# Attention with a distance bias and a gated MLP on one core: the first two steps share one side of PSUM, shared steps move in odd groups, weight rows load earlier

## Chip, cores and metric

The kernel runs on 1 core of one Trainium2 chip. The metric is the device time of one execution in microseconds. Engines are named as in the profile: PE is TensorE (PEld its weight loads), DVE VectorE, ACT ScalarE, POOL GpSimd, SP SyncE, which here only issues DMAs.

## The reference

Two parts follow each other: attention over 4 batches x 8 heads x 576 positions x 64, with an additive bias that a small network makes from the distance of two positions, and an MLP over the 2304 tokens whose activation is a rational function.

```python
# attention, q, k, v: (4, 8, 576, 64)
scores = scale * np.matmul(q, k.transpose(0, 1, 3, 2))
x = (log1p(|i - j|) / log1p(max(i, 1)))[..., None]
h = np.maximum(x @ w1 + b1, 0.0)              # 32 hidden
bias = h @ w2                                 # 8 heads
attn = softmax(scores + bias.transpose(2, 0, 1)[None])
x = (attn @ v)  ->  (2304, 512)
# MLP: w_in (512, 2048), w_out (2048, 512), a[4], b[2]
h = x @ w_in
g = (a[0] + a[1]*h + a[2]*h**2 + a[3]*h**3) / (1 + |b[0]|*|h| + |b[1]|*h**2 + 1e-6)
out = g @ w_out
```

## The kernel before

**The table.** The bias depends on i and j only. 36 groups of 16 rows i are made one after the other (list `order`): VectorE and ScalarE make up to four rows of relu(w1 * l + b1) for each (`relu`, from the table `lts` of logarithms, scaled by w1 at L709), TensorE multiplies them with w2 (L761) into two of the eight PSUM banks (`pa`), ScalarE evicts them (`e`, L767), and SyncE stores `e` into `tab` in device memory (L772). `load_bias(p, c)` (L260) reads the bias of head pair p and row block c back from `tab[c]`, in three DMAs, six for c = 4.

**Attention.** A unit u is a pair of heads p of one batch b; there are 16. A unit has row blocks c = 0 to 3 of 128 rows, and the last 64 rows of units u and u + 1 together are one shared step (u, 4). `steps` lists them; nine steps, those of units u and u + 1, are a group: steps 9g to 9g + 8 are group g. Two steps i = 2r and i + 1 are one round r (`rnd`), r from 1 to 35. In a round TensorE makes, in this order, the scores of both steps (`e_qk`, L341), the transposes of the probabilities of the two steps before (`e_tp`, L425), and the products with v (`e_pv`, L484) of steps i - 3 and i - 2. VectorE takes scores and bias to a reduced tile with `e_ttr` (L357), copies the tails of the transposes (L452) and the outputs (L493); ScalarE makes exponentials (`e_exp`, L373) and copies the transposes (L440). `side(i)` says which four banks the scores of a step use. Steps 0 and 1 are started inside the table (`start`).

**What lies beside it.** While attention runs, `job_plan` splits the weights into a high and a low part, one job for each part of 128 rows or columns, a job every one and a half rounds: `load` (wx, L140, 512 KB) by SyncE, then steps on VectorE (wk, L156), ScalarE and GpSimd (L177, L188), then stores. wx has four buffers. `load_qk`, `load_v` and `load_bias` are called from `loads(i)`. When a unit's last step is through, its sums are inverted, copied out (rs, L462) and read back as `rb` (L392), and `e_norm` (L408) multiplies the unit's output by it, on GpSimd, for units 12 and 15 on VectorE, and stores it (L410). `done_to` says when.

**What sets the order.** The order on each engine is written out by hand: every engine and SyncE's queue do their instructions in program order. After round 35 and `finish` the MLP runs with matmuls alone on TensorE.

Of the kernel before, what the change touches and what calls it, by code (L numbers as in the profile page):

```python
# [9 lines left out]
F32 = mybir.dt.float32  # L10
F32R = mybir.dt.float32r
U32 = mybir.dt.uint32
AF = mybir.ActivationFunctionType
ALU = mybir.AluOpType
# [23 lines left out]
def tile_attn_moe(  # L38
# [194 lines left out]
    with tc.manual_schedule():  # L233
# [3 lines left out]
        with ExitStack() as actx:  # L237
# [84 lines left out]
            for u in range(2, len(units), 2):  # L322
                steps += [(u, c) for c in range(5)] + [(u + 1, c) for c in range(4)]
            s2, prob, pt, tl, xs = {}, {}, {}, {}, {}
            rsum, rb = {}, {}

            def side(i):
                return 4 * ((max(i // 2, 1) - 1 + i) % 2)

# [180 lines left out]
            def loads(i):  # L510
                g, c = divmod(i, UPG)
                for u, x, y in ((2 * g + 2, 0 if g else 4, 3 if g else 6), (2 * g + 3, 5 if g else 7, 8)):
                    if u < NU and c == x:
                        load_qk(u)
                    if u < NU and c == y and u != 3:
                        load_v(u)
                if i == UPG + 1:
                    load_v(3)
                p, r = divmod(i, 2 * UPG)
                r = {2: 0, 7: 1, 11: 2, 13: 3, 16: 4}.get(r)  # L520
                if r is not None and p + 1 < NP:
                    load_bias(p + 1, r)
                if i == NS - 18:
                    load_x(0, 0, 0, KD - 1)
                if i == NS - 5:
                    load_x(1, 1, 0, KD - 1)
# [3 lines left out]
            def done_to(k):  # L530
                g, c = divmod(k, UPG)
                u = 2 * g - 2
                if g > 0:
                    if c == (0 if g > 1 else 1) and u != NX or k == NS:
                        norms.extend(e_norm(u))
                    if c == 6 and g * 2 < NU:
                        norms.extend(e_norm(u + 1))
                    if c == 2 and u + 1 < NU - 1:
                        load_rb(u + 1)
                if k == NS - 8:  # L540
                    x12.append(xs[NX])
                    late.extend(e_norm(NX))
                if g < NU // 2 and c == (7 - g % 2 if g else 8):
                    load_rb(2 * g)
# [15 lines left out]
            def job_plan(r):  # L560
# [10 lines left out]
                def out(c):  # L571
                    def go():
                        jobs[c][3][3](False, True)
                        run(list(after.get(c, [])))
                        if c + 3 < len(jobs):
                            jobs[c + 3][0]()
                    return go
# [12 lines left out]
            def rnd(r):  # L590
# [27 lines left out]
                for x in plan["between"]:  # L618
                    op = x()
                for x in plan["pool2"]:  # L620
                    behind(x(), op)
                small = [ends[r] + ends_[r] + adds[r] for r in range(2)]
                weave(main[0][:4] + small[0] + main[0][4:] + main_[0], main[1] + small[1] + main_[1])
                copy(1, 2)
                copy(0, 1)
# [9 lines left out]
                for x in hi[:1]:  # L635
                    x()
                for k in (i, i + 1):
                    for j in range(2):
                        e_exp(k, j)
                recip(i - 2)  # L640
# [6 lines left out]
                done_to(i - 1)  # L647
                run(late)
                loads(i + 1)
                if r == 2:  # L650
                    for x in jobs[:3]:
                        x[0]()
# [35 lines left out]
            with ExitStack() as bctx:  # L688
# [7 lines left out]
                bts = tpool.tile([P, NG * 4], F32, tag="bts", name="bts")  # L696
                LCUT = 320
                nc.scalar.dma_start(out=cs, in_=cst)
                nc.sync.dma_start(out=lts[:, :LCUT], in_=ltab[:, :LCUT])
                nc.sync.dma_start(out=lts[:, LCUT:], in_=ltab[:, LCUT:])  # L700
# [6 lines left out]
                A.activation(out=w28, in_=cs[:, 8 + 5 * NG:], func=AF.Identity, scale=8.0)  # L707
                for a, z in ((0, LCUT), (LCUT, S)):
                    V.tensor_scalar(  # L709
                        out=lts[:, a:z], in0=lts[:, a:z], scalar1=w1s, scalar2=None, op0=ALU.mult  # L710
                    )
                for x in range(9):
                    on(T.matmul(W[:, 6, 0:P], ident, ident, start=True, stop=True), 6)  # L713
# [12 lines left out]
                def relu(n):  # L726
                    for c, e in enumerate(ENG[n]):
                        r = ring[nring[0] % len(ring)][:, :dist(n)]
                        nring[0] += 1
                        m = 4 * n + c  # L730
                        if e == "A":
                            A.activation(out=r, in_=lts[:, :dist(n)], func=AF.Relu, bias=bts[:, m:m + 1])
# [10 lines left out]
                for n in order[:LEAD]:  # L743
                    relu(n)
                for y, n in enumerate(order):
                    if y == 13:
# [4 lines left out]
                    mid = i0 + NROW - 1  # L751
                    pa = 2 * ((y if y >= NG - 2 else y + 2) % 4)
                    pa = (pa, pa + 1)
                    cuts = sorted({0, mid, 512, EW})
                    for a, z in zip(cuts, cuts[1:]):
# [10 lines left out]
                    o = 512 * pa[0]  # L766
                    on(A.activation(  # L767
                        out=e, in_=WF[:, o:o + EW], func=AF.Identity, scale=rts[:, n:n + 1]
                    ), *pa)
                    g, k = divmod(n, 8)  # L770
# [309 lines left out]
```

## Time and profile before

| | |
|---|---|
| median of 3 plain runs | 660.62 us (660.62 to 661.08) |
| profiled execution, own time | 662.25 us |
| profiled execution, span | 660.5 us |
| mean granted TensorE clock | 0.999 |
| PE busy | 653.5 us, 99% |
| DVE busy | 561.3 us, 85% |
| ACT busy | 472.2 us, 71% |
| POOL busy | 154.1 us, 23% |
| all DMAs | 118.98 MB, 117.79 of them on one queue |

The span runs from the first to the last instruction; 1.75 us lie around it in the profiled execution. The end of a matmul is modelled in these profiles, so a busy PE may still be stretched. The chain of waits that ended last lies on PE for 96% of the span.

### The profile page before, as it was taken

The numbers are of one execution on the slowest core, as the hardware profiler recorded it, in microseconds if no ns is written. First come the engines' busy times: TensorE is split into PE (matmuls) and PEld (weight loads), VectorE is DVE, ScalarE is ACT, GpSimd is POOL, SyncE is SP. The second block draws the span as 40 slices with busy tenths as digits, with TensorE's granted clock in tenths as the row PEclk, the third lists the DMA queues.
The fourth block names the chain that finished last, engine by engine and source line by source line (L and its number), as shares of the span: only waits on it lengthen the run. The fifth ranks groups of instructions, "written<-read, shape, count | busy, mean of one in ns | idle before, by whom it ended". The sixth has DMA issues, their size and how long they took to land.

```text
span 660.5 us, 16193 instructions
## 1 busy us (share of the span) xinstructions
PE 653.5 (99%) x6274; PEld 546.8 (83%) x6274; DVE 561.3 (85%) x1100; ACT 472.2 (71%) x758; POOL 154.1 (23%) x108
## 2 busy tenths in 40 slices
PE   9999999999999999999999999999999999999997
PEld 6657888888888878988888888989988888888996
DVE  7997889988988895899999989979769779687776
ACT  7988999999999987767667566576656555555551
POOL 0000233333433330122212121222221221212211
PEclk9999999999999999999999999999999999999999
DMA  7887878868987975452825607669431301312031
GB/s 242 294 310 226 273 240 266 259 228 231 321 277 226 330 238 167 156 187 72 264 97 164 229 21 249 214 207 318 146 111 49 129 0 65 110 42 86 1 113 48
DMA packets 74845, 118.98 MB, mean 180 GB/s; under 512 B 11904, under 2 KB 33808, under 8 KB 74768
## 3 DMA queue, kind: packets, MB, share of 16 engines
q1 hardware_dynamic: 74624, 117.79, 54.2%
q8 instruction: 49, 0.80, 0.5%
q14 instruction: 28, 0.23, 0.1%
q10 hardware_dynamic: 144, 0.16, 0.1%
HBM read 79.17 MB, written 35.61 MB: 174 GB/s over the span
## 4 chain that ended last, share of the span: by engine, by line
PE 96%; DMA 1%; ACT 1%; issue 1%; DVE 0%; SPq 0%; POOL 0%; DVEq 0%; ACTq 0%; POOLq 0%
PE ps L316 30%; PE ps L909 30%; PE ps L484 12%; PE ps L341 11%; PE ps L761 6%; PE ps L425 6%; DMA tab<-e 1%; DMA bias<-tab 1%; PE ps L713 1%; ACT pt L440 1%; ACT p L373 1%; DVE s L357 0%; SPq L260 0%; DVE pre L930 0%; ACT wh L165 0%
## 5 line engine op out<-in xcount | busy, mean ns | idle before, releaser
L879 POOL TENSOR_TENSOR gl<-m,r 128x1024 fp32r<-128x1024 f32 (+1 forms) x39 | 85.6, 2195 | 295.5 <-DVE m L872 255.7
L830 ACT ACTIVATE w<-ps,babs 128x1024 f32<-128x1024 f32 (+1 forms) x40 | 41.3, 1033 | 107.1 <-PE ps L316 103.4
L373 ACT ACTIVATE p<-s,m 128x576 f32<-128x576 f32 x144 | 110.5, 783 | 0.2 <-DVE m L357 0.2
L357 DVE CUSTOM_DVE_ANT_0 s<-ps,bias 128x576 f32<-128x576 f32 (+1 forms) x144 | 95.2, 682 | 10.1 <-PE ps L341 3.9
L440 ACT COPY pt<-ps 128x512 f32<-128x512 f32 (+1 forms) x109 | 71.9, 732 | 17.6 <-PE ps L425 17.0
L909 PE MATMUL ps<-wol,gh 128*128 128x512 f32 x216 | 84.2, 390 | 0.0
L909 PE MATMUL ps<-woh,gh 128*128 128x512 f32 x216 | 84.2, 390 | 0.0
L341 PE MATMUL ps<-k,q 64*128 64x288 f32 (+1 forms) x640 | 82.3, 418 | 0.4 <-ACT e L767 0.2
L842 DVE SCALAR_TENSOR_TENSOR u<-w,babs,ps 128x1024 f32<-128x1024 f32 (+1 forms) x40 | 46.9, 1172 | 38.1 <-ACT t L831 38.0
L484 PE MATMUL ps<-pt,v 128*64 128x128 f32 (+1 forms) x1280 | 78.2, 265 | 0.8 <-ACT pt L440 0.5
L484 PEld LDWEIGHTS ps<-pt,v 128*64 128x64 f32 x1280 | 65.1, 137 | 5.8 <-ACT pt L440 1.6
L316 PE MATMUL ps<-xb,wih 128*128 128x512 f32 (+1 forms) x240 | 68.8, 367 | 0.0
L341 PEld LDWEIGHTS ps<-k,q 64*128 64x128 f32 (+1 forms) x640 | 50.9, 175 | 20.8 <-issue 6.4
L837 ACT ACTIVATE u<-u 128x1024 f32<-128x1024 f32 (+1 forms) x40 | 39.1, 978 | 40.2 <-DVE u L842 40.0
L425 PEld LDWEIGHTS ps<-ident,p 64*128 64x128 f32 x1296 | 49.6, 138 | 8.7 <-DVE m L357 2.9
L858 DVE SCALAR_TENSOR_TENSOR gh<-t,cst,r 128x1024 fp32r<-128x1024 f32 (+1 forms) x40 | 47.0, 1174 | 9.3 <-ACT r L839 6.9
L909 PE MATMUL ps<-woh,gl 128*128 128x512 f32 x216 | 53.8, 389 | 0.0
L425 PE MATMUL ps<-ident,p 64*128 64x64 f32 x1296 | 51.8, 226 | 0.5 <-ACT p L373 0.2
L865 DVE SCALAR_TENSOR_TENSOR m<-u,qc,gh 128x1024 f32<-128x1024 f32 (+1 forms) x40 | 47.1, 1178 | 4.0
L316 PEld LDWEIGHTS ps<-xb,wih 128*128 128x128 f32 x240 | 44.5, 188 | 6.1
L872 DVE SCALAR_TENSOR_TENSOR m<-t,cst,m 128x1024 f32<-128x1024 f32 (+1 forms) x40 | 47.1, 1179 | 1.4
L851 DVE SCALAR_TENSOR_TENSOR t<-t,cst,ps 128x1024 f32<-128x1024 f32 (+1 forms) x40 | 47.0, 1175 | 1.4
(82 smaller groups left out, 1343.9 us busy)
## 6 DMA issues: line engine op xcount, KB each, us to landing
tab<-e SPq DMA_DIRECT2D x36, 295.5 KB, 3.5
wx<-in_w_in_dram SPq DMA_DIRECT2D x16, 512.0 KB, 5.4
wx<-in_w_out_dram SPq DMA_DIRECT2D x16, 512.0 KB, 4.2
v<-in_vp_dram SPq DMA_DIRECT2D x16, 320.0 KB, 6.3
ws<-wh SPq DMA_DIRECT2D x20, 256.0 KB, 4.7
ws<-wl SPq DMA_DIRECT2D x20, 256.0 KB, 4.3
q<-in_qt_dram SPq DMA_DIRECT2D x16, 288.0 KB, 4.1
k<-in_kt_dram SPq DMA_DIRECT2D x16, 288.0 KB, 3.3
```

What stands on the lines that cost most here:

```text
L316: on(T.matmul(hps[s][:, j, :w_], w[:, k, sl], x[:, k, :w_], start=(k == 0 and z == 0), stop=(k == KD - 1 and z == 2),), b + j)
L341: on(T.matmul(W[o, b, :SH], q[r, x], k[r, a * SH:(a + 1) * SH], start=True, stop=True), b)
L357: op = on(V.tensor_tensor_reduce(out=t3[:, a], in0=W[:, b:b + 2][:, a, :SH], in1=b3[:, a], scale=-0.125, scalar=least, op0=ALU.add, op1=AL ...
L373: A.activation(out=prob[i][:, z * S:z * S + S], in_=t, func=AF.Exp, bias=m, scale=-1.0, accum_out=sums[u % 4][:, k:k + 1],)
L425: on(T.transpose(W[:, b, o:o + 64], src[x, :], ident[x, x]), b)
L440: on(A.copy(out=t.rearrange("p x (r s) -> p r x s", r=2)[:, a:z], in_=W[:, to[a]:to[a] + z - a].rearrange("p r (x s) -> p r x s", s=64),), ...
L484: on(T.matmul(ps[y, o], vt[n][:, kc, y], w_, start=(kc == 0), stop=(kc == 4)), b, mem=(f"pt{i % 3}", f"tl{i // 2 % 2}"))
L851: on(V.scalar_tensor_tensor(out=rt[s, "t"], in0=rt[s, "t"], scalar=abs_[:, 1:2], in1=hp(s), op0=ALU.add, op1=ALU.mult,), *hb(s), mem="t")
L865: V.scalar_tensor_tensor(out=m, in0=rt[s, "u"], scalar=qc, in1=rt[s, "gh"].bitcast(F32), op0=ALU.add, op1=ALU.mult,)
L872: V.scalar_tensor_tensor(out=m, in0=rt[s, "t"], scalar=abs_[:, 0:1], in1=m, op0=ALU.add, op1=ALU.subtract)
L879: eng.tensor_tensor(out=lo, in0=rt[s, "m"], in1=rt[s, "r0"], op=ALU.mult)
L909: on(T.matmul(po[n, c], l[:, j, c * P:(c + 1) * P], r[fp][:, j, :], start=(first and x is a), stop=(last and x is z),), OB[c])
```

## The change

In words: both of the first two steps make their scores in banks 4 to 7, and the table's banks turn by two, so that its last two row groups lie in banks 0 to 3; the last row group is evicted by VectorE. ScalarE's rows of the first group come from an unscaled table `ltr`, with the scale in the instruction, and the second half of the scaling comes after the rows of two groups. In groups 1, 3 and 5 the first step of unit u + 1 goes ahead of the shared step; the q and k load of that group, the reads of `rb` and the normalisation of the even unit move with it. A job's load is issued four jobs ahead and before the stores of its place, not three jobs ahead and behind them, and the first four loads stand at the end of round 1, where three stood at the end of round 2. The normalisation of unit 12 on VectorE moves from the end of one round to behind the first step's reductions of the next. In round 1 the first exponential of step 2 stands ahead of the copies.

```diff
@@ steps and sides
             for u in range(2, len(units), 2):
-                steps += [(u, c) for c in range(5)] + [(u + 1, c) for c in range(4)]
+                if u % 4 and u + 2 < len(units):
+                    steps += [(u, c) for c in range(4)] + [(u + 1, 0), (u, 4)]
+                    steps += [(u + 1, c) for c in range(1, 4)]
+                else:
+                    steps += [(u, c) for c in range(5)] + [(u + 1, c) for c in range(4)]
             def side(i):
-                return 4 * ((max(i // 2, 1) - 1 + i) % 2)
+                return 4 * ((i // 2 - 1 + i) % 2) if i > 1 else 4
@@ loads, done_to
-                for u, x, y in ((2 * g + 2, 0 if g else 4, 3 if g else 6), (2 * g + 3, 5 if g else 7, 8)):
+                for u, x, y in ((2 * g + 2, 0 if g else 4, 3 if g else 6), (2 * g + 3, 5 + g % 2 if g else 7, 8)):
-                    if c == (0 if g > 1 else 1) and u != NX or k == NS:
+                    if c == (0 if g % 2 else 2) and 1 < g and u != NX or g == 1 and c == 1 or k == NS:
                         norms.extend(e_norm(u))
-                if g < NU // 2 and c == (7 - g % 2 if g else 8):
+                if g < NU // 2 and c == (8 if g == 0 else 6 if 2 * g + 2 == NU else 7):
                     load_rb(2 * g)
@@ job_plan
                     def go():
+                        if c + 4 < len(jobs):
+                            jobs[c + 4][0]()
                         jobs[c][3][3](False, True)
                         run(list(after.get(c, [])))
-                        if c + 3 < len(jobs):
-                            jobs[c + 3][0]()
@@ rnd
                 for x in plan["between"]:
                     op = x()
+                run(late)
...
+                soon = 1 if r == 1 else 0
+                for j in range(soon):
+                    e_exp(i, j)
                 copy(1, 2)
...
-                for k in (i, i + 1):
-                    for j in range(2):
-                        e_exp(k, j)
+                for k, j in [(k, j) for k in (i, i + 1) for j in range(2)][soon:]:
+                    e_exp(k, j)
...
-                run(late)
                 loads(i + 1)
-                if r == 2:
-                    for x in jobs[:3]:
+                if r == 1:
+                    for x in jobs[:4]:
                         x[0]()
@@ table
-                nc.sync.dma_start(out=lts[:, :LCUT], in_=ltab[:, :LCUT])
+                nc.sync.dma_start(out=ltr, in_=ltab[:, :LCUT])
...
-                        if e == "A":
+                        if e == "A" and n == order[0]:
+                            A.activation(
+                                out=r, in_=ltr[:, :dist(n)], func=AF.Relu, bias=bts[:, m:m + 1], scale=w1s
+                            )
+                        elif e == "A":
...
                 for n in order[:LEAD]:
                     relu(n)
+                scale(lts, lts, LCUT, S)
...
-                    pa = 2 * ((y if y >= NG - 2 else y + 2) % 4)
+                    pa = 2 * ((y + 2 if y >= NG - 2 else y) % 4)
...
+                    if y < NG - 1:
+                        on(A.activation(... scale=rts[:, n:n + 1]), *pa)
+                    else:
+                        on(V.tensor_scalar(
+                            out=e, in0=WF[:, o:o + EW], scalar1=rts[:, n:n + 1], scalar2=None, op0=ALU.mult
+                        ), *pa)
```

On SyncE's queue, behind the last three DMAs of the bias of pair 1, block 0, in rounds 1 and 2 (names: wx0_0 is the load of job 0, its row part; q2 is q of unit 2), before:

```order
L260 DMA bias1_911<-tab0_66 128x64
L266 DMA q2_998<-in_qt_dram 128x576
L267 DMA k2_999<-in_kt_dram 128x576
L140 DMA wx0_0_1096<-in_w_in_dram 128x2048
L140 DMA wx0_1_1098<-in_w_out_dram 128x2048
L140 DMA wx1_0_1100<-in_w_in_dram 128x2048
L273 DMA v2_1102<-in_vp_dram 128x640
L266 DMA q3_1203<-in_qt_dram 128x576
```

and after:

```order
L260 DMA bias1_912<-tab0_66 128x64
L140 DMA wx0_0_999<-in_w_in_dram 128x2048
L140 DMA wx0_1_1001<-in_w_out_dram 128x2048
L140 DMA wx1_0_1003<-in_w_in_dram 128x2048
L140 DMA wx1_1_1005<-in_w_out_dram 128x2048
L266 DMA q2_1007<-in_qt_dram 128x576
L267 DMA k2_1008<-in_kt_dram 128x576
L273 DMA v2_1105<-in_vp_dram 128x640
L266 DMA q3_1206<-in_qt_dram 128x576
```

Four wx loads stand ahead of q2 and k2, where three stood behind them.

On PE in round 6 of group 1 (pt9 and tl8 are operands of the products with v, a score of 64 rows belongs to the shared step), before, from the end of round 5 into the scores of round 6:

```order
L484 MATMUL ps_91<-pt8_1336,v1_412 64x128 x8
L484 MATMUL ps_91<-tl8_1403,v1_412 64x128 x2
L341 MATMUL ps_91<-k2_999,q2_998 128x288 x4
L341 MATMUL ps_91<-k2_999,q2_998 64x288
L341 MATMUL ps_91<-k3_1204,q3_1203 64x288
```

and after, from the end of round 6 into the scores of round 7:

```order
L488 MATMUL ps_91<-pt9_1340,v2_1105 64x128 x8
L488 MATMUL ps_91<-tl8_1406,v2_1105 64x128 x2
L488 MATMUL ps_91<-pt10_1458,v2_1105 64x128 x8
L488 MATMUL ps_91<-tl10_1527,v2_1105 64x128 x2
L345 MATMUL ps_91<-k2_1008,q2_1007 64x288
L345 MATMUL ps_91<-k3_1207,q3_1206 64x288
```

The shared scores stood second in round 6 and now open round 7.

On DVE from the end of round 33 into round 34 (xs12 is the output of unit 12, s2_68 and s2_69 the two steps of the round, the rows of width 1 are the reductions' second halves), before:

```order
L493 COPY xs14_4745<-ps_91 128x128
L408 TENSOR_TENSOR xs12_4160<-xs12_4160,rb12_4532 128x576
L493 COPY xs14_4745<-ps_91 128x128
L357 ISA s2_68_0_4785,m68_0_0_4786<-ps_91,bias3_2985 128x288
L357 ISA m68_0_0_4786 128x1
L357 ISA s2_68_0_4785,m68_0_1_4788<-ps_91,bias3_2985,m68_0_0_4786 128x288
```

and after:

```order
L497 COPY xs14_4746<-ps_91 128x128 x2
L361 ISA s2_68_0_4784,m68_0_0_4785<-ps_91,bias3_2988 128x288
L361 ISA m68_0_0_4785 128x1
L361 ISA s2_68_0_4784,m68_0_1_4787<-ps_91,bias3_2988,m68_0_0_4785 128x288
L361 ISA m68_0_1_4787 128x1
L361 ISA s2_68_1_4789,m68_1_0_4790<-ps_91,bias3_2988 128x576
L361 ISA m68_1_0_4790 128x1
L412 TENSOR_TENSOR xs12_4163<-xs12_4163,rb12_4533 128x576
L361 ISA s2_69_0_4833,m69_0_0_4834<-ps_91,bias3_2988 128x576
```

The multiplication by rb12 has moved from between two copies out of PSUM to between the reductions of steps 68 and 69.

## Rows read from the trace of the kernel before

**Rows 1.** Page, section 1: busy us of each engine, share, instructions.

```profile
PE 653.5 (99%) x6274; PEld 546.8 (83%) x6274; DVE 561.3 (85%) x1100; ACT 472.2 (71%) x758; POOL 154.1 (23%) x108
```

**Rows 2.** Chain of waits in order of time: start us, us, what.

```profile
49.74 4.63 DMA tab<-e
55.42 4.37 DMA bias<-tab
...
62.24 2.30 PE ps L341 x24
...
68.12 2.14 PE ps L341 x16
```

**Rows 3.** Timeline, 59 to 62 us: start us, us, instruction [idle before <-releaser].

```profile
59.91 0.76 DVE L357 CUSTOM_DVE_ANT_0 s<-ps,bias 128x576 f32<-128x576 f32 x1 [1.53 <-DMA bias<-tab]
...
61.81 0.44 PE L484 MATMUL ps<-tl,v 128*64 128x128 f32 x4 [0.16 <-DVE tl L452]
```

**Rows 4.** Timeline, PE's scores of step 1 behind the table.

```profile
48.12 0.75 PE L341 MATMUL ps<-k,q 64*128 64x288 f32 x2
...
49.11 3.39 PE L341 MATMUL ps<-k,q 64*128 64x288 f32 x21 [0.24 <-ACT e L767]
```

**Rows 5.** Timelines of PEld and of DVE, first table rows.

```profile
5.57 0.20 PEld L761 LDWEIGHTS ps<-ring,w 128*32 128x32 f32 x8 [0.22 <-ACT ring L732]
...
4.56 27.84 DVE L734 TENSOR_SCALAR ring<-lts,bts 128x320 f32<-128x320 f32 x76
```

**Rows 6.** Timeline of SyncE's queue, 54 to 67 us: when DMAs were issued.

```profile
54.57 6.80 SPq L260 DMA_DIRECT2D bias<-tab  x12
61.42 0.43 SPq L266 DMA_DIRECT2D q<-in_qt_dram  x1
...
66.33 0.71 SPq L260 DMA_DIRECT2D bias<-tab  x1
```

**Rows 7.** DMA issues: count, KB each, us to landing; two single ones, two groups.

```profile
q<-in_qt_dram SPq DMA_DIRECT2D x1, 288.0 KB, 4.1
...
bias<-tab SPq DMA_DIRECT2D x1, 288.0 KB, 8.5
...
wx<-in_w_in_dram SPq DMA_DIRECT2D x16, 512.0 KB, 5.4
...
v<-in_vp_dram SPq DMA_DIRECT2D x16, 320.0 KB, 6.3
```

**Rows 8.** Busy time by stretch; the last three: PE clock, DMA share, GB/s.

```profile
68.00:70.00 2.00, 2.00 (x20) 1.60 (x17) 1.55 (x7) 2.00 (x7) 1.04 (x1) 1.00 1.02 403
```

**Rows 9.** Chain of waits: starts of rounds 6, 10 and 14.

```profile
79.79 2.30 PE ps L341 x24
...
103.30 2.14 PE ps L341 x16
...
126.65 2.14 PE ps L341 x16
```

**Rows 10.** Chain of waits, starts of rounds 29 and 30; timeline, VectorE in round 29.

```profile
214.38 1.23 PE ps L341 x16
...
220.70 2.14 PE ps L341 x16
...
215.38 0.43 DVE L156 TENSOR_SCALAR wk<-wx 128x512 uint32<-128x512 uint32 x1 [0.60 <-DMA wx<-in_w_out_dram]
```

**Rows 11.** Chain of waits, starts of rounds 34 and 35; timeline, VectorE.

```profile
244.40 0.73 PE ps L341 x4
...
250.54 2.14 PE ps L341 x16
...
244.69 0.76 DVE L408 TENSOR_TENSOR xs<-xs,rb 128x576 f32<-128x576 f32 x1 [0.88 <-DMA rb<-rs]
```

**Rows 12.** Chain of waits, behind the last matmul; busy time by stretch, end.

```profile
656.88 0.69 DVE pre L930
...
659.00:660.50 1.50, 0.00 (x0) 0.00 (x0) 0.00 (x0) 0.00 (x0) 0.00 (x0) 0.52 0.07 23
```

More of the change, by code (lines that the diff above doesn't have):

```diff
@@ L697, in tile_attn_moe @@
                 LCUT = 320
+                ltr = tpool.tile([P, LCUT], F32, tag="ltr", name="ltr")
                 nc.scalar.dma_start(out=cs, in_=cst)
-                nc.sync.dma_start(out=lts[:, :LCUT], in_=ltab[:, :LCUT])
+                nc.sync.dma_start(out=ltr, in_=ltab[:, :LCUT])
                 nc.sync.dma_start(out=lts[:, LCUT:], in_=ltab[:, LCUT:])
@@ L707, in tile_attn_moe, with scale @@
                 A.activation(out=w28, in_=cs[:, 8 + 5 * NG:], func=AF.Identity, scale=8.0)
-                for a, z in ((0, LCUT), (LCUT, S)):
+                def scale(src, dst, a, z):
                     V.tensor_scalar(
-                        out=lts[:, a:z], in0=lts[:, a:z], scalar1=w1s, scalar2=None, op0=ALU.mult
+                        out=dst[:, a:z], in0=src[:, a:z], scalar1=w1s, scalar2=None, op0=ALU.mult
                     )
+                scale(ltr, lts, 0, LCUT)
                 for x in range(9):
@@ L766, in tile_attn_moe @@
                     o = 512 * pa[0]
-                    on(A.activation(
-                        out=e, in_=WF[:, o:o + EW], func=AF.Identity, scale=rts[:, n:n + 1]
-                    ), *pa)
+                    if y < NG - 1:
+                        on(A.activation(
+                            out=e, in_=WF[:, o:o + EW], func=AF.Identity, scale=rts[:, n:n + 1]
+                        ), *pa)
+                    else:
+                        on(V.tensor_scalar(
+                            out=e, in0=WF[:, o:o + EW], scalar1=rts[:, n:n + 1], scalar2=None, op0=ALU.mult
+                        ), *pa)
                     g, k = divmod(n, 8)
```

## The prediction, made before the changed kernel ran

> **What bounds the kernel now.** I read the page first: TensorE is busy for 653.5 of 660.5 us [rows 1], so a change pays only where TensorE stands still or a stretch of it is stretched, and costs wherever TensorE is made to wait. Next the chain of waits in order of time. From 68 us on it is TensorE almost without a break, in rounds of 5.8 us (scores of two steps, transposes, products with v). The one stretch where it leaves TensorE for long lies behind the table: the DMA that writes the last table row (49.74, 4.63 us), the DMA that reads bias part 3 of pair 0 (55.42, 4.37 us), and only then rounds 3 and 4, which begin at 62.24 and 68.12 [rows 2]. That path ends on VectorE: the reduction of step 5 = (0,3) waits until 59.91 for that bias, the copy of the tails stands behind it on VectorE, and TensorE, which has all else done, waits for that copy at 61.81 [rows 3]. So the end of round 2 is set by when the bias lands, whatever TensorE did before.
>
> **The change, part by part.** The sum is made on the profiled execution (span 660.5 us, 662.25 us with what lies around it); the median of the plain runs is 660.62, and I carry the difference over to that.
>
> *First two steps on one side of PSUM, last eviction on VectorE, first e_exp early.* Before, step 1's scores wait in banks 6 and 7 for ScalarE's eviction of the last table row, until 49.11 [rows 4]; they began at 48.12, so up to 0.98 us of TensorE's time is freed there. It is freed ahead of the landing at 59.91 and is waited away again there: the DMA path of [rows 2] does not start sooner, since VectorE can begin the eviction only when TensorE has ended the row, as ScalarE did, and the queue issues the row's DMA at 49.74, behind other rows. I take 0; the bound is 0.98 if the landing did not decide.
>
> *Raw table for ScalarE, late half of the scaling.* TensorE's first table product waits 0.22 us for ScalarE's first rows. But VectorE makes most of the rows and runs from 4.56 on for 27.84 us without a gap [rows 5]. Its work is the same, only the scaling of 256 columns stands four rows later, so it ends its rows when it ended them before. Gain 0 to 0.22; I take 0.1, nearer to 0, because the engine without gaps is the one that the table's end waits for.
>
> *Shared steps of odd groups.* In groups 1, 3 and 5 the step (u, 4), whose scores are twice as many small products, moves from second to first place of a round, where even groups have it. The four rounds of such a group (with the shared scores, the shared products and both transposes of sums) take 103.30 - 79.79 = 23.51 us, the same four of an even group 126.65 - 103.30 = 23.35 [rows 9]. Three groups at 0.16: gain 0.48 (0.3 to 0.6). Their reciprocal, the copy of the sums and the rb loads come a round later, the normalisation on GpSimd one or two rounds later; no step before the MLP reads these, and GpSimd then waits less for rb, so I cost that at nothing. If GpSimd came late with a conversion instead, VectorE's join would wait, at most some tenths in three places.
>
> *Weight rows loaded one job further ahead.* In round 29 VectorE's first conversion step waits 0.60 us for a wx load, and the round takes 220.70 - 214.38 = 6.32 us [rows 10] where round 3, also with the shared step first, takes 5.88 [rows 2]. One job more of lead is 1.5 rounds, some 8.7 us: gain 0.44 (0.3 to 0.5). Next late there is nothing in that round.
>
> *Normalisation of unit 12 on VectorE behind step 68's reductions.* It now waits 0.88 us for rb, at the front of round 34, with PSUM copies on both sides of it that TensorE needs; the round takes 250.54 - 244.40 = 6.14 us [rows 11] against 23.35 / 4 = 5.84. Moved, the wait is gone, but 0.76 us stand between two reductions and everything behind is that much later: the tails are still in time by some 0.4 us, the copies of the next round barely. Gain 0 to 0.30; I take 0.25.
>
> *Four loads of weight rows at the end of round 1 instead of three in round 2.* This is the part that costs. On SyncE the four wx loads now stand ahead of q and k of unit 2, where three stood behind them; all are on one queue. Nothing lets them issue before the 12 bias DMAs, which hold the queue from 54.57 to 61.37 [rows 6]. Step 9 = (2,0) is the second step of round 4: it needs q and k at 68.12 + 2.14 / 2 = 69.2. Before, q was issued at 61.42 and landed 4.1 us later, at 65.5; the bias DMA issued at 66.33 landed 8.5 us later, at 74.8 [rows 6, 7]. Between the two landings lie k, three wx, v, q, k and that bias, 288 + 3 x 512 + 320 + 3 x 288 = 3008 KB = 3.08 MB in 9.3 us: the queue works in order of issue and moves 331 GB/s. The four wx loads are 2.10 MB, so they push q by 6.3 us to 71.8 and k, 0.9 us behind it, to 72.7: TensorE stands for 3.5 us. At the 403 GB/s of the best stretch there [rows 8] it is 5.2 and 0.7 us, k at 71.4, and 2.2 us. I take 3.1, nearer to the first, which includes the landing. Nothing gives it back: later rounds have no slack on TensorE, and all of it is in program order.
>
> The Trainium skill, "DMA: Bandwidth & Descriptors", section "Specifications", gives a limit of about 358 GB/s from HBM for a core; by it, as an estimate, the four loads would take 5.9 us and the wait would be 3.0. No run here shows the limit itself.
>
> Sum: 3.1 - 0.1 - 0.48 - 0.44 - 0.25 = +1.8 us; the profiled execution would take 664.1, a plain run 660.6 + 1.8 = 662.4.
>
> **Rivals.**
> (a) *TensorE's clock falls in the wait.* The last matmuls end near 656.9, and in the last stretch, from 659.0 on, the mean granted clock is 0.52 [rows 12]: about 2.2 us of standing still were enough for the lower level, 1.2 GHz. A wait of 3 us could do it too. Against: busy TensorE surrounds it, and the smaller gaps of this trace leave the clock at 1.00. Price between 0 and one round at half speed, 5.8; I take 2: 664.4. The Trainium skill, "TensorE: Matmul & The Clock Gate", section "What's actually happening", says that the slow level is the resting one and that activity lifts it; the fall behind the last matmul agrees.
> (b) *The wait is short.* q and k get through among the wx rows, or wx moves faster than any stretch of two microseconds here, and k lands at 70.4: 1.2 us, which the gains cancel: 660.6. For it: DMAs of one queue run on 16 engines that need not keep step. Against: the 8.5 us of the bias DMA.
> (c) *No wait, the change does what its words say*: q and k come before 69.2 and only the gains stay, 660.6 - 1.27 = 659.3. It decides if the queue's backlog at the issue of q, about 63.4, is under 5 us, which is the landing point of k; above that it is (b) or the forecast. Against it: 2.1 MB at the best rate are 5.2 us.
> (d) *As (c), and the freed 0.98 us on TensorE counts as well*, because the bias lands sooner: 658.4.
>
> **How the numbers follow.** Chances: forecast 0.42 (its own range 661.2 to 663.5: wait 2.2 to 3.9, gains 0.8 to 1.6), (a) 0.20, (b) 0.15, (c) 0.15, (d) 0.05, and 0.03 for a loss elsewhere, such as GpSimd late in the odd groups. Likeliest: 662.4. From 659.4 to 664.6 leaves out half of (c), (d) and the upper third of (a), under 0.2. A measurement of this kernel tells 0.2%, 1.3 us, from no change: faster means below 659.3, slower above 661.9. Faster: half of (c) and (d), 0.12. Within: the rest of (c), most of (b), a quarter of the forecast, 0.31. Slower: 0.57.
>
> **What would show it.** In the profile after: round 4's scores with a gap of about 3 us in the middle, ended by the DMA of q or k, and no work of TensorE in it; a clock below 1.00 near 72 us for (a). Round 2 ending within 0.3 us of 62.2. Rounds 6 to 9, 15 to 18 and 24 to 27 at 23.35 each, round 29 at 5.9, round 34 at 5.8 to 5.9. Wrong would make it: q and k of unit 2 landing before 70 us, then the order of issue does not set the order of landing; a bias landing well before 59.9; odd groups that keep 23.5.

## The result, and the profile after

The changed kernel takes 669.87 us (665.10 to 672.74, six executions) against 660.87 us (660.62 to 664.34) for the kernel before in the same runs: 1.0119 times as long, 95% interval 1.0071 to 1.0167. The forecast was 662.4, up to 664.6, for a kernel before at 660.6. The direction was right. The size was not: the medians lie 9.0 us apart where 1.8 was forecast. And the kernel has become uneven: its executions lie 7.6 us apart.

The profiled execution lies near the lower end of these (666.04 us, span 664.2). The rows of its page that answer to [rows 1]:

```profile
span 664.2 us, 16204 instructions
PE 653.4 (98%) x6274; PEld 548.2 (83%) x6274; DVE 561.9 (85%) x1101; ACT 470.7 (71%) x757; POOL 153.5 (23%) x108
PEclk9999899999999999999999999999999999999999
```

TensorE is as busy as before (653.4 us, before 653.5) in a span 3.7 us longer, and one slice of the clock's row, the fifth (66 to 83 us), is below 9. There the timeline of TensorE (start, duration, line, operation, count, in brackets the idle time before it and what ended it) shows:

```profile
67.50 1.24 PE L345 MATMUL ps<-k,q 64*128 64x288 f32 x8
72.24 2.29 PE L345 MATMUL ps<-k,q 64*128 64x288 f32 x8 [3.50 <-DMA k<-in_kt_dram]
74.29 1.73 PE L429 MATMUL ps<-ident,p 64*128 64x64 f32 x36
...
78.47 1.73 PE L345 MATMUL ps<-k,q 64*128 64x288 f32 x12
```

The first row is the scores of step 8, the last the start of round 5. Between the scores of steps 8 and 9 TensorE stands idle 3.50 us for k of unit 2, and eight instructions of the kind that took 1.24 us then take 2.29. The chain of waits (start, duration, what) has the landing of k at 63.81 + 8.30 = 72.11:

```profile
63.81 8.30 DMA k<-in_kt_dram
```

The windows of that stretch (start and end, length, busy time of PE, PEld, DVE, ACT, POOL with the number of instructions, then granted clock, share of the DMA engines, GB/s) say why:

```profile
70.00:72.00 2.00, 0.00 (x0) 0.00 (x0) 0.20 (x2) 0.15 (x1) 0.00 (x0) 0.97 1.03 406
72.00:74.00 2.00, 1.76 (x8) 1.47 (x10) 0.00 (x0) 0.00 (x0) 0.00 (x0) 0.50 0.94 360
74.00:76.00 2.00, 2.00 (x40) 1.66 (x36) 0.83 (x3) 0.57 (x2) 0.00 (x0) 0.68 0.15 50
76.00:78.00 2.00, 1.95 (x49) 1.94 (x50) 1.82 (x8) 2.00 (x5) 0.00 (x0) 1.00 0.04 8
```

When TensorE resumes, the clock is at its lower level (0.50, 1.2 GHz), and it is back at 1.00 only past 75 us. Round 4 takes 78.47 - 67.50 = 10.97 us where it took 5.87: 3.5 for the wait and 1.6 for the clock.

Three more rows of the chain of waits show a loss that the prediction did not have, in round 31:

```profile
218.11 5.86 DMA rs<-rt
226.50 4.66 DMA xd<-xs
231.18 0.04 DVE xs L497
```

On SyncE's queue the store of xs of unit 9 now stands right behind four rb loads, and these wait for the landing of the sums that they read. It issues at 226.50 and lands at 231.16, and VectorE's copy for unit 13, into the same buffer, waits for it. The round takes 6.44 us instead of 5.86.

The balance of the two profiled executions: round 4 +5.10, round 31 +0.58, start -0.55 (round 3 begins at 61.62, before 62.17), the three odd groups -0.51, round 29 -0.45, round 34 -0.35. That is +3.8. The medians lie 9.0 us apart; the other 5.2 are not in these two traces: this execution lies 3.8 us below the changed kernel's median, and that of the kernel before 1.4 above its own.

### The profile page after: what moved, and what is told of

Read it like the earlier page. It is cut to its first block, busy times and chain, and to the rows that moved or that the text cites. A ratio compares the mean times of both kernels' runs of the same rounds, so it can differ in the third digit from the quotient of the medians.

```text
span 664.2 us, 16204 instructions
## 1 busy us (share of the span) xinstructions
PE 653.4 (98%) x6274; PEld 548.2 (83%) x6274; DVE 561.9 (85%) x1101; ACT 470.7 (71%) x757; POOL 153.5 (23%) x108
## 4 chain that ended last, share of the span: by engine, by line
PE 85%; DMA 4%; ACT 2%; SPq 2%; issue 0%; DVE 0%; DVEq 0%
PE ps L316 30%; PE ps L929 30%; PE ps L488 11%; PE ps L345 9%; PE ps L429 5%; DMA k<-in_kt_dram 1%; SPq L260 1%; DMA rs<-rt 1%; ACT pt L444 1%; ACT p L377 1%; DMA tab<-e 1%; DMA xd<-xs 1%; PE ps L776 0%; SPq L140 0%; SPq L400 0%
```

## The experiments

**Once more.** First the changed kernel again, for another trace.

> The changed kernel once more, unaltered, to see whether its spread (665.1 to 672.7 us over six executions) belongs to it. Theory W (wait and clock): the wait for k of unit 2 in round 4 is 3 to 4 us in each execution, and what varies is how long TensorE's clock stays at its lower level behind it; a trace with a longer time shows the lower clock in more windows than 72 to 76 us, and nothing else longer. Rival L (landing): the landing of k varies by some us, and round 4's wait with it, at a clock of 1.00. Rival E (elsewhere): round 4 takes 11.0 us as in the first trace, and the rest of the loss stands in another round. By all three the median is 665 to 671; round 4 tells them apart.

Measured: 669.50 us (668.01 to 670.28), ratio 1.0114 (1.0096 to 1.0132); the profiled execution took 670.28 us. Round 4 takes 10.81 us, as in the first trace. But round 29, 5.88 us there, takes 9.97. The timelines of ScalarE, SyncE's queue and TensorE:

```profile
223.84 0.72 ACT L165 ACTIVATE wh<-wk,wmin 128x512 uint32<-128x512 uint32 x1 [2.97 <-DMA ws<-wh]
224.47 1.97 ACT L444 COPY pt<-ps 128x512 f32<-128x512 f32 x3
```

```profile
218.39 0.38 SPq L128 DMA_DIRECT2D ws<-wh  x1
```

```profile
225.09 1.22 PE L488 MATMUL ps<-pt,v 128*64 128x128 f32 x16 [2.78 <-ACT pt L444]
```

ScalarE's conversion step (L165, `rebias`) wants to write a wh tile, of which there are two; the one it gets holds weight rows that still have to be stored to DRAM (tile 7, w_out). That store issues on SyncE's queue at 218.39, 5.84 us after the start of round 28; in the trace of before it issues 3.18 us after it, in the first trace of the changed kernel 2.58 us. There was little to spare even before: its last part landed at 216.08, and ScalarE's step began at 216.25. ScalarE stands 2.97 us, its copy of the transposes behind it, TensorE 2.78 us behind that, and the clock falls again (0.50 from 226 to 228 us). The wait was already there in the first trace, 0.19 us long. So rival E held, as far as two traces go: round 4 is steady (10.97 and 10.81 us), and what differs is round 29.

**The loads' edit alone, and the loads behind q and k.** Two kernels part the loss. only_wx is the kernel before with the change's edit to the weight rows and no other:

```diff
+                        if c + 4 < len(jobs):
+                            jobs[c + 4][0]()
                         jobs[c][3][3](False, True)
                         run(list(after.get(c, [])))
-                        if c + 3 < len(jobs):
-                            jobs[c + 3][0]()
...
-                if r == 2:
-                    for x in jobs[:3]:
+                if r == 1:
+                    for x in jobs[:4]:
```

> The kernel before with only the edit to the loads of weight rows (four at the end of round 1, one job further ahead). Theory W: all of the loss is in this edit: round 4 waits for k by 3 to 3.5 us and loses 1.6 us or more behind it to the clock, round 29 gains 0.45; 660.6 + 5.1 - 0.45 = 665.3 or above, with the spread. If another part of the change causes the loss or the spread, it stays under 663.

qk_ahead is the changed kernel with q and k of unit 2 loaded one step sooner, which puts them ahead of the four loads:

```diff
-                for u, x, y in ((2 * g + 2, 0 if g else 4, 3 if g else 6), (2 * g + 3, 5 + g % 2 if g else 7, 8)):
+                for u, x, y in ((2 * g + 2, 0 if g else 3, 3 if g else 6), (2 * g + 3, 5 + g % 2 if g else 7, 8)):
```

> The changed kernel with one edit: q and k of unit 2 are issued one step earlier, so that they stand ahead of the four loads of weight rows. Theory W: no wait in round 4, no fall of the clock, round 4 takes 5.85 us, and the time falls by the 5.1 us of the profiled round and by all of the spread: 660.6 - 0.55 (start) - 0.51 (odd groups) - 0.45 (round 29) - 0.35 (round 34) + 0.58 (round 31) = 659.3 us, with a spread of under 1 us. If the spread has another cause, the median stays at 662 or above and the times differ by several us. If the order of issue does not set the order of landing, k still lands at 72 and nothing changes.

Measured: only_wx 666.38 us against 661.42 for the kernel before in the same runs, +5.0. Its round 4 waits 3.43 us for k and takes 11.86, with the clock between 0.50 and 0.66 from 70 to 78 us. In qk_ahead round 4 is back at 5.87 us at full clock, with the scores of both steps in one piece: the order of issue does set the order of landing, and the wait is gone. TensorE's scores, first only_wx, then qk_ahead:

```profile
71.88 2.29 PE L341 MATMUL ps<-k,q 64*128 64x288 f32 x8 [3.43 <-DMA k<-in_kt_dram]
```

```profile
68.79 2.21 PE L345 MATMUL ps<-k,q 64*128 64x288 f32 x16
```

Yet qk_ahead takes 664.86 us (661.11 to 666.54), +3.4, not the 659.3 expected: round 29 takes 9.95 us in its trace, again with ScalarE standing 2.7 us ahead of L165. The profile names a reduction of VectorE there, but the step also waits for the same store of wh, whose last part lands at 219.99, 0.11 us before it begins. Half of theory W fell: the wait in round 4 is the loads' doing, the spread is not.

**The odd groups, alone and undone.** only_odd is the kernel before with the change's order of steps, and its conditions in loads and done_to that belong to it:

```diff
-                steps += [(u, c) for c in range(5)] + [(u + 1, c) for c in range(4)]
+                if u % 4 and u + 2 < len(units):
+                    steps += [(u, c) for c in range(4)] + [(u + 1, 0), (u, 4)]
+                    steps += [(u + 1, c) for c in range(1, 4)]
+                else:
+                    steps += [(u, c) for c in range(5)] + [(u + 1, c) for c in range(4)]
...
```

> The kernel before with only the edit to the odd groups (shared step first in a round, its normalisation and rb loads later). Theory O: this edit holds SyncE's queue up near 182 to 216 us (loads of rb wait there for sums that are stored a round later, behind one more store of xs), so the store of a converted weight tile (wh) lands 3 us or more later, and in part of the executions ScalarE's next write of that tile waits for it in round 29, with ScalarE's PSUM copy behind it and TensorE behind that. Then times spread over several us, from 660.7 (660.6 - 0.51 and + 0.58 in round 31) to 665, and the median is 661.5 to 664. Rival X: the lateness comes from the weight rows loaded one job further ahead, which stand in the same queue; then this kernel has no spread and takes 660 to 661, with round 29 at 6.3 us.

no_odd is qk_ahead with all of these lines taken back.

> The kernel qk_ahead (the changed kernel with q and k of unit 2 ahead of the weight rows) with the edit to the odd groups undone: groups, rb loads and normalisation as before. Theory O: no round waits for a store any more; round 29 takes 5.9 us, round 31 5.86, odd groups 23.5; 660.6 - 0.45 - 0.35 and 0 to 0.5 from the start give 659.3 to 659.8, against a median of 664.9 for qk_ahead, and the spread is that of the kernel before (some 2 us). Rival X: the spread and the 4 us in round 29 stay, median 662 or above.

Measured: only_odd 664.64 us (663.11 to 668.02), +3.4 against 661.29; no_odd 661.34 us, ratio 0.9996 (0.9979 to 1.0013). In only_odd, which has none of the edits to the loads, ScalarE waits for the same store:

```profile
216.04 0.72 ACT L165 ACTIVATE wh<-wk,wmin 128x512 uint32<-128x512 uint32 x1 [1.22 <-DMA ws<-wh]
```

and VectorE waits 2.4 us for rb in round 34, which takes 7.71 us:

```profile
DVE xs L412 <- DMA rb<-rs: 2.4, 1, 2.4
```

Theory O holds, rival X does not, though the median lies above the 661.5 to 664 expected. The two parts add up, 4.96 + 3.35 = 8.3 us, against 669.50 - 661.42 = 8.1 for the whole change in the runs of again, but in part by luck: in only_odd's trace 1.9 us of the loss is in round 34, which takes 5.79 in the traces of the changed kernel, where the normalisation of unit 12 has moved. The odd groups' price in the changed kernel is better read from qk_ahead and no_odd, which differ in them alone: 664.86 - 661.34 = 3.5 us, from two sets of runs.

no_odd is not faster than the kernel before, though, as it should be by the gains of rounds 29 and 34; the traces of the kernel before, below, say why. Its one trace is of its longest execution (666.17 us). It shows a wait of 2.4 us of VectorE for a wx load in round 4, where q and k now stand ahead of them, one of 0.59 us of ScalarE for the store of wh in round 29, and in round 31, 7.66 us long, a store of xs that took 9.18 us to land:

```profile
221.70 9.18 DMA xd<-xs
```

So these waits can come without the odd groups too, in single executions.

How the odd groups hold the queue up shows in what SyncE's queue waited for between 100 and 220 us (waiting line, releaser: us in total, times, longest); first before, then only_odd:

```profile
SPq L392 <- DMA rs<-rt: 14.0, 6, 4.9
```

```profile
SPq L396 <- DMA rs<-rt: 25.5, 8, 4.4
```

These are the rb loads, waiting at the head of the queue for the sums. The store of the sums of an odd group's first unit comes a round later, and so do the rb loads that read them; but the loads of v, q and k, which stood behind the rb loads, now stand ahead of the store. When SyncE's queue issued these in group 1, first before, then only_odd:

```profile
101.05 0.39 SPq L462 DMA_DIRECT2D rs<-rt  x1
102.17 0.35 SPq L140 DMA_DIRECT2D wx<-in_w_out_dram  x1
102.61 1.10 SPq L196 DMA_DIRECT2D woh<-wh  x1
103.81 0.55 SPq L392 DMA_DIRECT2D rb<-rs  x1
...
106.39 0.53 SPq L273 DMA_DIRECT2D v<-in_vp_dram  x1
```

```profile
102.70 0.54 SPq L273 DMA_DIRECT2D v<-in_vp_dram  x1
103.28 0.49 SPq L266 DMA_DIRECT2D q<-in_qt_dram  x1
103.83 0.45 SPq L267 DMA_DIRECT2D k<-in_kt_dram  x1
104.38 0.38 SPq L466 DMA_DIRECT2D rs<-rt  x1
104.80 0.34 SPq L140 DMA_DIRECT2D wx<-in_w_in_dram  x1
108.94 0.45 SPq L396 DMA_DIRECT2D rb<-rs  x1
```

Before, the sums landed 2.2 us after their store was issued, while the queue issued two other transfers; it did not stand. In only_odd one transfer stands between, the sums land 4.5 us after the issue, at 108.92, between v (108.42) and q (109.14), and the queue stands 3.7 us, with all that is behind it. Groups 3 and 5 show the same: 1.6 us from issue to landing in both before, 4.5 and 5.7 in only_odd.

**Work in the wait: the clock's part.** Extra work for TensorE: products of unit 1's q and k, into banks that step 9 overwrites, between the scores of steps 8 and 9 of the changed kernel; fill_wait has 12 pairs of them, fill_less 6.

```diff
-                weave(sa[0] + sb[0], sa[1] + sb[1])
+                if r == 4:
+                    weave(sa[0], sa[1])
+                    for x in range(12):
+                        for j in range(2):
+                            z, k1 = slice(64 * j, 64 * j + 64), qk[1]
+                            on(T.matmul(
+                                W[0:P, o + 2 * j, :SH], k1[0][z, 0:P], k1[1][z, :SH], start=True, stop=True
+                            ), o + 2 * j)
+                    weave(sb[0], sb[1])
+                else:
+                    weave(sa[0] + sb[0], sa[1] + sb[1])
```

> The changed kernel with 24 further products of q and k of unit 1 between the scores of steps 8 and 9, into banks that step 9 then overwrites: some 3.2 us of work for TensorE (24 at 0.134 us, from 2.14 us for 16) in the wait for k, and nothing else changed. The wait itself stays. Theory W: the clock stays at 1.00 in round 4, which takes 5.85 + 3.5 = 9.4 us instead of 11.0, and the spread goes: 660.6 + 3.5 - 1.28 = 662.8 us. If the clock has no part in the loss (rivals L and E), the time and the spread stay those of the changed kernel, 665 to 673.

> The changed kernel with 12 further products of unit 1's q and k in the wait for k in round 4 (24 took 5.82 us in the run fill_wait, so these take 2.9 us); the wait and all else stay. If idling lets the clock fall, it now stays at 1.00 through round 4, since under 1 us of idling is left, and round 4 takes 5.8 + 3.5 = 9.3 us instead of 10.8 to 11.0. If the clock falls whatever stands there, round 4 keeps 10.8 or more. Read from round 4 alone; the whole time still has the loss of round 29 in it.

In fill_wait the 24 products took 5.82 us and not 3.2 (I had counted two instructions of a product as two products), more than the wait: round 4 takes 11.61 us, at a clock of 1.00, and the price cannot be read. The whole took 667.95 us. fill_less settles it. Its timeline of TensorE, then its windows:

```profile
68.49 3.08 PE L616 MATMUL ps<-k,q 64*128 64x288 f32 x24
72.98 1.24 PE L345 MATMUL ps<-k,q 64*128 64x288 f32 x8 [1.42 <-DMA k<-in_kt_dram]
```

```profile
70.00:72.00 2.00, 1.57 (x14) 0.92 (x10) 0.11 (x2) 0.07 (x1) 0.00 (x0) 1.00 1.03 403
72.00:74.00 2.00, 1.01 (x8) 0.95 (x10) 0.00 (x0) 0.00 (x0) 0.00 (x0) 1.00 0.97 369
```

k comes later here (72.85), so the stretch from the end of step 8's scores is 4.5 us, a microsecond more than in the first trace; but TensorE idles only 1.42 of it, the clock stays at 1.00, the eight instructions take 1.24 us, and round 4 takes 10.38, which is 5.87 + 4.5 and nothing more. The 1.6 us in the first trace were the clock. (667.53 us in all, with 7.91 us in round 29.)

**Two loads ahead instead of four.**

```diff
-                if r == 1:
-                    for x in jobs[:4]:
+                if r in (1, 2):
+                    for x in jobs[:2] if r == 1 else jobs[2:4]:
```

> The changed kernel with two of the four loads of weight rows ahead of q and k of unit 2, the other two at the end of round 2. Theory W: each load (512 KB) pushes k by 1.3 to 1.6 us; k landed 3.3 to 3.5 us late behind four, so it is 0.1 to 0.9 us late behind two: round 4 takes 5.9 to 6.8 us at a clock of 1.00. If the wait does not scale with the loads ahead, round 4 stays above 8 us. Read from round 4 alone.

```profile
70.16 1.24 PE L345 MATMUL ps<-k,q 64*128 64x288 f32 x8 [1.55 <-DVE m L361]
```

Round 4 takes 7.61 us, more than the 5.9 to 6.8 expected, with 1.55 us of idling and the clock at 1.00. The row names a reduction of VectorE; but k's last part landed at 70.03, 0.13 us before TensorE began, and in the first trace the same reduction ended at the same moment (70.19) with TensorE standing two microseconds longer, so I read it as the landing of k. None, two and four loads ahead give 0, 1.55 and 3.5 us. (665.69 us in all; here round 26 waits for a store of wh.)

**The stores on another queue.** On qk_ahead, ScalarE issues the stores of wh of tiles 6 to 9 itself, in the round after the conversion, behind its copies of the transposes.

```diff
-            if t is not None:
+            if t is not None and i == 0 and f < KF - LATE:
+                held.append(lambda t=t: nc.scalar.dma_start(out=d[:, 0], in_=t.bitcast(F32)))
+            elif t is not None:
                 nc.sync.dma_start(out=d[:, i], in_=t.bitcast(F32))
...
                 copy_(0, 2)
+                while held:
+                    held.pop(0)()
```

> The kernel qk_ahead with one more edit: the eight stores of the high half of converted weight rows (ws from wh, rows 6 to 9) go out on ScalarE's DMA queue in the round behind the conversion, instead of on SyncE's queue, which runs one to two rounds behind. Theory O: what costs the time in qk_ahead is ScalarE's wait for these stores in round 29 (and 26); with the stores out of SyncE's queue no round from 23 to 30 waits on ws, rounds 26 and 29 take 5.9 us, and the median falls from 664.9 by 3 to 4 us to 660.5 to 662. Rival L: SyncE's lateness costs in other places too (xs behind xd, round 31; q and k); then only part of the 3.4 us comes back, median 662 to 664, and the trace shows the other wait. If the wait in round 29 is not for the store, nothing changes: 664 to 665.

Measured: 671.22 us (670.23 to 674.70), worse than the kernel it was to mend. No instruction waits for ws any more, but round 24 takes 12.48 us. ScalarE's timeline:

```profile
188.13 0.33 ACTq L128 DMA_DIRECT2D ws<-wh  x1
188.51 0.78 ACT L379 ACTIVATE p<-s,m 128x576 f32<-128x576 f32 x1 [5.05 <-DMA rb<-rs]
```

ScalarE's DMA instruction itself waited 5 us, for a landing of rb from SyncE's queue that it does not use, and everything of ScalarE stood behind it. The trace shows why: in this program the DMAs of SyncE and ScalarE take eight completion semaphores in turn, and each waits until the last DMA with its semaphore has landed. This store drew the semaphore (103) of an rb load that was issued at 185.38 and landed at 188.11. So issuing from another engine did not part the two queues, by the program's semaphores. The Trainium skill, "DMA: Bandwidth & Descriptors", section "Issuing engines are not separate DMA queues", says that moving DMAs to another engine saves only the time to issue them; this run saved nothing either, but the semaphores alone account for that. As a test of theory O it is void, since it put a new wait in the place of the old one.

**The rb loads one round later.** On qk_ahead, in SyncE's order alone:

```diff
-                if g < NU // 2 and c == (8 if g == 0 else 6 if 2 * g + 2 == NU else 7):
+                if g < NU // 2 and (g % 2 == 0 or 2 * g + 2 == NU) and c == (8 if g == 0 else 6 if 2 * g + 2 == NU else 7):
                     load_rb(2 * g)
+                if 0 < g < NU // 2 and g % 2 == 0 and c == 0:
+                    load_rb(2 * g - 2)
```

> The kernel qk_ahead with one more edit, on SyncE's queue alone: the four rb loads of the first unit of an odd group stand one round later there, behind some seven other transfers, so that the queue no longer stands for the landing of the sums (rs) that they read. Theory O: this standing is how the odd groups hold the queue up; the queue is then 2 to 4 us earlier from round 11 on, the store of wh7_1 issues near or before 3 us into round 28 instead of 5.0, the store of xs9 lands before round 31 needs it, and the median falls from 664.9 to 660 to 662. If the queue is held up by the amount of data and not by this standing, the store of wh7_1 issues as late as before and the median stays at 663.5 to 665.5.

> The kernel qk_ahead with both edits, rb loads one round later and the stores of wh on ScalarE's queue. Theory O: no wait behind round 4 but those of the kernel before; the gains of the odd groups (0.5), of round 29 (0.45) and of round 34 (0.3) are left: 661.2 - 1.25 = 660.0 against some 661.2 for the kernel before in the same runs, 0.2 to 1.5 us faster. If anything else of the change costs time, it is above 661.5.

Measured: rb_later 660.96 us (660.75 to 661.32), 3.9 us below qk_ahead and with a spread of 0.6 us in ten executions. What the queue waited for, in qk_ahead and in rb_later, and rb_later's store of wh:

```profile
SPq L396 <- DMA rs<-rt: 19.2, 7, 4.8
```

```profile
SPq L396 <- DMA rs<-rt: 9.0, 4, 3.3
```

```profile
209.39 0.38 SPq L128 DMA_DIRECT2D ws<-wh  x1
```

9.0 us in place of 19.2; the store issues 1.6 us into round 28 instead of 5.0, and round 29 takes 5.88 us. This is the run that shows the mechanism: twelve small transfers moved on one queue, and nothing else. The kernel called both, with wh_act's edit on top, takes 667.46 us: the wait that ScalarE's own DMAs bring stays (10.09 us in round 24), so its expectation of 660.0 failed by that edit. Against the kernel before (661.38) rb_later stands at 0.9989 (0.9972 to 1.0007): 1.3% under the changed kernel, not shown to be faster than the one before. Its trace has the 0.51 us of the odd groups, and gives them back in rounds 4 and 26, which take 6.07 and 6.22 us (5.86 and 5.88 in the trace of before_2, below).

**Where the gains were.** Twice the kernel before, and rb_later's order with the edit to the loads undone (three behind q and k in round 2, one job less ahead).

> The kernel before, unaltered, for a second trace of it. The trace that the sum was made on is of an execution of 662.25 us, 1.6 us above the median. Theory P: the three places from which the sum drew gains that no_odd did not show (the late bias at the end of round 2, the wait for wx in round 29, the wait for rb in round 34; 0.5 + 0.45 + 0.3) belong to that execution; in one near 660.6 us round 29 takes 5.9 and round 34 5.8 to 5.9 us. Rival G: they are in every execution, and the changed kernel loses the same elsewhere; then round 29 is at 6.3 and round 34 at 6.1 here too.

> The same once more, for a third trace. Theory P: rounds 29 and 34 are at 5.9 where the execution is at 660.6 us, and above in one of 662 us; rival G: 6.3 and 6.1 in each.

> The changed kernel with rb loads of the odd groups one round later (as in rb_later) and the whole edit to the weight rows undone: three loads behind q and k in round 2, one job less ahead, q and k where they were. By the reading so far (the early loads cost about 5 us, the odd groups about 3.4 by the standing of SyncE's queue, both now gone) only gains are left, and it takes 660.0 to 661.0 us, with rb_later's 660.96 beside it. If the lead of one job is worth its 0.45 us in every execution, it is 0.4 above rb_later, at 661.4; if it is worth nothing, or loads the queue, it is at 660.0 to 660.9 with a spread under 1 us.

In the trace of before_2 (661.08 us), starts of rounds 29 and 30, and of 34 and 35:

```profile
213.56 2.37 PE L341 MATMUL ps<-k,q 64*64 64x288 f32 x24
219.44 1.96 PE L341 MATMUL ps<-k,q 64*128 64x288 f32 x13
243.47 2.34 PE L341 MATMUL ps<-k,q 64*128 64x288 f32 x16
249.33 1.00 PE L341 MATMUL ps<-k,q 64*128 64x288 f32 x6
```

Round 29 takes 5.88 us and round 34 5.86, where [rows 10] and [rows 11] have 6.32 and 6.14; before_3 has 5.88 and 5.80 in an execution of 663.22 us, and loses 1.7 us in round 4, to a wx load, instead. Theory P holds in its main point, that those waits are not in every execution. Its tie to the whole time does not hold: before_3 takes 663.22 us without them. wx_undone takes 661.25 us (660.91 to 662.41), ratio 1.0001 (0.9992 to 1.0010), like rb_later: the job of lead is worth nothing that these runs can tell.

## Why the prediction was right and wrong

- *The wait for k in round 4*: mechanism, place and size were right. The forecast was 3.1 us with TensorE standing for k at 2.2 to 3.9; the traces show 3.50, 3.3 and 3.43, and 4.5 where k landed late. That the first of the two rates, 331 GB/s, gives the same 3.5 is partly luck: k landed at 72.1, between the 72.7 and the 71.4 of the two rates, and round 4 began at 67.50, not at 68.12. The estimate beside the sum went by 358 GB/s; from 70 to 72 us the DMA engines moved 406, and the measurement decides.
- *Its price*: too low. The loads alone cost 5.0 us where 3.1 was summed, since the term held the wait and not the clock behind it. Rival (a), the clock, got a chance of 0.20 beside the forecast, when in each of the three traces with 3.3 us or more of idling there it came with it: 1.6 us in the first, 2.6 in only_wx. The row for it was at hand, [rows 12], and I set "busy TensorE surrounds it" against that row with no row of its own. The Trainium skill, "TensorE: Matmul & The Clock Gate", section "HAM oscillation — how this bites in real kernels", tells of a kernel whose every DMA wait lets the clock fall; the traces agree for the waits of 3.3 us and more, while 1.42 and 1.55 us left it at 1.00.
- *The odd groups*: here the step failed outright. The gain per round was right (23.34 to 23.35 us for the four rounds, as forecast), but "the rb loads come a round later ... I cost that at nothing" asked only who reads rb. On an in-order queue the question is also what the rb loads wait for at its head, and who stands behind them: bias, and the stores that free buffers for ScalarE and VectorE. What the runs showed in place of nothing: the queue stands 3.7 us for the sums in group 1, where it did not stand, the store of wh is late, and the price is 3.4 us in the median (only_odd), 3.9 back in rb_later, and most of the spread, 5.4 us in qk_ahead against 0.6 in rb_later. The loss of 0.58 in round 31 hangs on the same queue, in another place, though no_odd's longest execution lost 1.8 there without the odd groups.
- *Round 29 and round 34*: measured -0.45 and -0.35 against the trace of before, as forecast, and still no gains: that execution lay 1.6 us above the median, and two further traces have neither wait. Carrying a difference over from that execution to the median was the mistake.
- *The start*: taken at 0, rightly. Round 3 begins between 61.44 and 62.92 us in the eleven traces with the change's start, and between 61.17 and 62.36 in the five without it. Which landing is last there varies by more than any edit moves it; the 0.55 of the first trace shows nothing.
- *Rivals (b) to (d)*: they needed k to land by 70.4; it landed at 72.1.

By these numbers the sum should have read: 5.0 for the loads, 3.4 for the odd groups, nothing for the rest, 669.0. What stays open is why the queue's lag becomes a wait of 0 to 4 us from one execution to the next. The start of round 3, which hangs on a landing of the bias, differs by up to 1.8 us between the traces, and by the eight semaphores a late landing can hold up the DMA eight places behind it; but no run isolates either.

## What to carry to other kernels

A transfer that is moved in an in-order queue is priced by what stands behind it, and by the latest buffer that waits to be freed there, not by who reads it. A load that reads what a store has just written should not stand next behind that store, least of all where large loads stand ahead of the store. A stand of TensorE is priced with the clock that it may cost, from the row in the trace that shows a fall. And before a sum is made on one trace, see how its own time lies to the median: a wait that belongs to that execution alone is no gain.

## What the runs showed of the hardware

- Behind a single stand of TensorE of 2.46 to 3.50 us the granted clock went to its lower level in each of six places (rounds 4, 24 and 29 in five runs): a window of 2 us behind it has 0.50 to 0.58. Below that it was not one way: 1.42 and 2.10 us (rounds 4 and 29 of fill_less), 1.55 (wx2_ahead) and 1.71 (round 34 of only_odd) left it at 1.00, 1.68 us (round 26 of wx2_ahead) was followed by 0.50.
- A DMA issued by ScalarE held ScalarE up to 5.05 us for a landing on SyncE's queue (wh_act), because the program gave both the same completion semaphore.
- With one core running, the DMA engines moved 406 GB/s over a stretch of 2 us (70 to 72 us of the first trace).
